# A gated scan with a mixture of experts: an earlier merge, masks with places in the order, another gather split

## The chip, the cores and the metric

The kernel runs on one core of a Trainium2 chip. The metric is device time in microseconds (us) of one launch. A core has a matrix engine (TensorE, PE in the profile, whose weight loads are shown as PEld), VectorE (DVE), ScalarE (ACT), GpSimd (POOL) and SyncE (SP, which here only issues DMAs).

## The reference

`x`, `r_gate` and `i_gate` are [4, 5056, 256] in fp32. First comes a gated linear recurrence along the sequence, then a top-1 mixture of experts over the 20,224 tokens that it gives:

```python
a = exp(8 * sigmoid(r_gate) * log(clip(sigmoid(a_param))))
u = sqrt(max(1 - a*a, 1e-6)) * sigmoid(i_gate) * x
h[t] = a[t] * h[t-1] + u[t]                      # for each of 4 sequences; y = h
logits = y @ w_gate                              # [20224, 8]
e = argmax(logits); gate = softmax(logits)[e]
for each expert: keep the 80 tokens with the largest gate
    out[token] = gate * (relu(y[token] @ w1[e]) @ w2[e])   # w1 256x1024, w2 1024x256
out of all other tokens = 0
```

At most 640 rows of the output are not zero.

## The kernel before

**Stages.** The tokens are cut into 40 units of 512 (unit 39 has 256). The outputs y of the recurrence stay on the chip, transposed, in the first 40 slots of one big tile `Y`; ten more slots and the free ones of the 40 hold what is loaded or under way. For each unit the program loads `r`, `i` and `x` (`Lr`, `Li`, `Lx`), transposes r on TensorE (`Tr`), makes the decay and the root on ScalarE and GpSimd, gates x, transposes it (`Tu`, two halves), multiplies by the norm on VectorE (`xg`) and scans on VectorE (`y`, two halves, line 173). Groups of four units get their logits on TensorE (`G`, for the last group `Ga` and `Gb`), and ten small stages (`R`, with a step number and a stage 0 to 9) turn logits into a table `rows`: one row for each of 16 slices of the tokens and each of the 8 experts, with the gate weight of each token that chose the expert. Step 4 is the last group but one, step 5 the last.

**The merge.** `P0` to `P3` (lines 324 to 328) keep the 8 largest of each 256 columns of the first 1024 columns of `rows`, 32 in all, in `cell`. `M0` (`merge(0)`, lines 334 to 338) takes the 16 largest of those 32 on VectorE and compares their positions with a list (line 338). `M1` and `M2` (lines 340 to 350) look up the columns on GpSimd. M0 keeps its positions in `pos`, which lies in slot 48 of `Y`; slot 48 also holds the loaded x of unit 38, which `Tu38.0` and `Tu38.1` read.

**The order.** The string `ORDER` (lines 35 to 64) lists all this, task by task, and each engine runs its own instructions in that order (`manual_schedule`, line 367). Its end, before:

```
u38.1 R3.8 y36.0 e38.1 Z y36.1 Tr39 R3.9 Tu37.1 tr39 xg37.0 G8 Z e39.1 q38.1 xg37.1 W0 s38.1 y37.0 q39.1 W1 y37.1 u39.1 P3 W2 Tu38.0 Tu38.1
s39.1 xg38.0 W3 R4.0 Tu39.0 xg38.1 R4.1 y38.0 W4 y38.1 Tu39.1 Z R4.2 Ga xg39.0 R4.3 xg39.1 y39.0 Z y39.1 W5 R4.4 R4.5 Gb Ca M0 W6 R5.0 R5.1
W7 R5.2 M1 R4.6 R5.3 R5.4 Z R5.5 R4.7 R5.6 M2 R4.8 Z R5.7 R5.8 R4.9 R5.9
```

`W` loads weights of the first two experts and `Z` zeroes 512 rows of the output; both are DMAs of SP's queue. What stands behind the list is placed by the compiler's scheduler. Among it are masks of constants (lines 383 to 390): `se` (written by GpSimd at line 383, finished by VectorE at 384 and 385), `iot` (386) and `comb` (389 and 390, VectorE).

**The choice.** Behind the list VectorE takes the 16 largest of the rest of `rows` (line 439), and lines 441 to 481 rank the candidates of the 16 slices against each other and turn the ranks into a table `chosen` of 80 tokens for each expert. Line 455 issues `WARM[0]` matmuls that compute nothing wanted (`keep_warm`, lines 418 to 420, tile `pd`).

**The experts.** `experts` (line 529) makes `col` (line 540), the columns of the 80 tokens of each expert in `Y`. For each expert, ScalarE, GpSimd and VectorE each load their share of the 80 columns into registers (`fetch`, line 553) and copy the tokens into `XG` one by one (`copies`, lines 559 and 560); `GATHER` gives the shares, 28, 24 and 28. Line 543 issues `WARM[1]` more empty matmuls in the meantime. Before the loop, VectorE turns a second table `pt` into `AT` (the gates) and `sidx` (the rows for the scatter) in six small instructions, lines 594 to 600. The loop (lines 603 to 616) gathers expert k+2, multiplies expert k+1 by w1 (`ph`, line 574) and expert k by w2 (`po`, line 576), interleaved, loads later weights as buffers come free, scales (line 584) and scatters (line 587).

Of the kernel before, what the change touches and what calls it, by code (L numbers as in the profile page):

```python
# [7 lines left out]
F32 = mybir.dt.float32  # L8
I32 = mybir.dt.int32
# [13 lines left out]
WARM = (7, 7)  # L23
GATHER = (28, 24, 28)
# [36 lines left out]
    u38.1 R3.8 y36.0 e38.1 Z y36.1 Tr39 R3.9 Tu37.1 tr39 xg37.0 G8 Z e39.1 q38.1 xg37.1 W0 s38.1 y37.0 q39.1 W1 y37.1 u39.1 P3 W2 Tu38.0 Tu38.1  # L61
    s39.1 xg38.0 W3 R4.0 Tu39.0 xg38.1 R4.1 y38.0 W4 y38.1 Tu39.1 Z R4.2 Ga xg39.0 R4.3 xg39.1 y39.0 Z y39.1 W5 R4.4 R4.5 Gb Ca M0 W6 R5.0 R5.1
    W7 R5.2 M1 R4.6 R5.3 R5.4 Z R5.5 R4.7 R5.6 M2 R4.8 Z R5.7 R5.8 R4.9 R5.9
# [18 lines left out]
def moe_kernel(ctx, tc, x, r_gate, i_gate, a_param, w_gate, w1, w2, out, capacity=80):  # L82
# [277 lines left out]
    def weights(w):  # L360
# [5 lines left out]
             'Tu': u_transposes, 'xg': normed, 'y': scan, 'G': logits, 'R': lambda s, k: stages[k](s), 'Ga': logits_first, 'Gb': logits_last, 'Ca': copy_first, 'P': cell_top, 'M': merge, 'W': weights, 'Z': lambda: zero_fill(1)}  # L366
# [14 lines left out]
    V = 2 * E  # L381
    se = lg[:, :P]; iot = lg[:, P:P + 80]
# [146 lines left out]
    def experts(arm):  # L529
        fstack = ExitStack()  # L530
        tstack = ExitStack()
        ps_t = tstack.enter_context(tc.tile_pool(name="ps_a" + arm, bufs=1, space=bass.MemoryType.PSUM))
# [8 lines left out]
        pt = ps_t.tile([CAP, 2 * E], F32, name="sel")  # L541
# [61 lines left out]
        for k in range(-1, E):  # L603
# [8 lines left out]
            if k >= 1: scatter(k - 1)  # L612
# [42 lines left out]
```

## Time and profile before

| | us |
|---|---|
| median of 3 runs (all of them) | 315.87 (315.51, 315.87, 318.1) |
| the profiled execution, its own time | 315.17 |
| its span, first to last instruction | 313.4 |
| busy in the span: PE, PEld | 217.6, 162.8 |
| DVE, ACT, POOL | 228.1, 233.0, 228.5 |

A page of the profile gives such sums, and other views list single instructions or groups of them by engine in order of time: start, duration, engine, line, operation, the tiles written and read with their shapes, how many there are (x8), and in brackets how long the engine had been idle before and what ended that. PEclk, the granted clock of TensorE, is given as a share of 2.4 GHz: 1.00 is that and 0.50 is 1.2 GHz. A TensorE row of fp32 matrices counts two instructions for a matmul and one for a transpose.

### The profile page before, as it was taken

Reading aid. Unit: us, or ns where it says so; the run is one execution under the profiler, and the core shown is the slowest. Engines: PE = TensorE matmul, PEld = TensorE weight load, DVE = VectorE, ACT = ScalarE, POOL = GpSimd, SP = SyncE. Lnnn points to the kernel's source line nnn. Section 1 sums busy time; section 2 is a strip of 40 time slices with the busy share of each in tenths; the row PEclk is TensorE's granted clock in tenths of the full one; section 3 lists DMA queues with packets and bytes.
Section 4 is the critical chain, followed back from the end, with each engine's and each line's share of the span. In section 5 each row is a group of like instructions: output and inputs, shape, how many; then the busy total and the mean of one; then the engine's idle time right before and its main releaser. Section 6 shows DMA issues by size and latency. Waiting matters only on the chain.

```text
span 313.4 us, 5668 instructions
## 1 busy us (share of the span) xinstructions
PE 217.6 (69%) x1404; PEld 162.8 (52%) x1404; DVE 228.1 (73%) x541; ACT 233.0 (74%) x463; POOL 228.5 (73%) x370
## 2 busy tenths in 40 slices
PE   3571677776456971988645957569618879999993
PEld 3451664426345241934633433344205669999993
DVE  1052699799989995999499996797968554666520
ACT  6999969999999996998899998898115353545400
POOL 2469298899999889799996999797257465654612
PEclk9958577959959997599795788756956598999999
DMA  7989999999999599989978999998999133999941
GB/s 254 405 310 391 395 337 413 407 390 391 413 405 351 188 386 389 395 310 367 393 291 321 349 383 338 383 330 278 360 423 335 55 101 131 331 341 344 315 128 29
DMA packets 32824, 100.73 MB, mean 321 GB/s; under 512 B 3744, under 2 KB 12576, under 8 KB 32160
## 3 DMA queue, kind: packets, MB, share of 16 engines
q1 hardware_dynamic: 32400, 99.64, 86.5%
q0 software_dynamic: 384, 0.66, 0.6%
q8 instruction: 13, 0.21, 0.3%
q14 instruction: 27, 0.22, 0.2%
HBM read 99.10 MB, written 21.36 MB: 384 GB/s over the span
## 4 chain that ended last, share of the span: by engine, by line
issue 25%; POOL 21%; DMA 14%; DVE 13%; PE 13%; ACT 9%; POOLq 2%; DVEq 1%; SPq 1%; ACTq 0%
DMA Y<-in_i_gate_dram 6%; POOL Y L143 6%; POOL Y L155 5%; DMA Y<-in_r_gate_dram 4%; POOL Y L154 4%; PE pr L126 4%; PE pl L236 4%; DVE pu L165 4%; ACT Y L140 3%; DMA Y<-in_x_dram 3%; POOL Y L560 3%; DVE Y L173 3%; PE pu L162 2%; ACT Y L128 2%; POOLq L553 2%
## 5 line engine op out<-in xcount | busy, mean ns | idle before, releaser
L173 DVE TENSOR_TENSOR_SCAN Y<-Y,pu 128x512 f32<-128x512 f32 (+4 forms) x86 | 97.2, 1170 | 0.0
L143 POOL TENSOR_TENSOR Y<-Y 128x1024 f32<-128x1024 f32 (+2 forms) x30 | 74.3, 2489 | 26.9 <-ACT Y L140 25.4
L162 PE MATMUL pu<-ident,Y 128*128 128x128 f32 x316 | 57.8, 322 | 39.3 <-DVE Y L173 24.2
L162 PEld LDWEIGHTS pu<-ident,Y 128*128 128x128 f32 x316 | 42.2, 166 | 65.6 <-issue 25.2
L126 PE MATMUL pr<-ident,Y 128*128 128x128 f32 x316 | 54.2, 332 | 30.3 <-DMA Y<-in_r_gate_dram 19.7
L155 POOL TENSOR_TENSOR Y<-Y 128x1024 f32<-128x1024 f32 (+2 forms) x25 | 68.7, 2747 | 4.5 <-DMA Y<-in_x_dram 2.5
L126 PEld LDWEIGHTS pr<-ident,Y 128*128 128x128 f32 x316 | 46.9, 175 | 33.9 <-issue 16.8
L165 DVE SCALAR_TENSOR_TENSOR pu<-Y,pu 128x512 f32<-128x512 f32 (+1 forms) x80 | 51.3, 676 | 14.5 <-ACT Y L146 7.5
L140 ACT ACTIVATE Y<-Y,tiny 128x512 f32<-128x512 f32 (+2 forms) x60 | 53.1, 943 | 1.5 <-DVE Y L157 1.2
L576 PE MATMUL po<-Y,rows 128*80 128x128 f32 x256 | 47.7, 279 | 0.0
L574 PE MATMUL ph<-Y 128*128 128x80 f32 x256 | 43.5, 262 | 2.2 <-DVE Y L560 2.0
L128 ACT ACTIVATE Y<-pr 128x1024 f32<-128x1024 f32 (+1 forms) x40 | 38.9, 1003 | 3.8 <-PE pr L126 3.8
L150 ACT ACTIVATE Y<-Y 128x1024 f32<-128x1024 f32 (+2 forms) x30 | 38.8, 1320 | 3.8 <-DMA Y<-in_i_gate_dram 3.2
L574 PEld LDWEIGHTS ph<-Y 128*128 128x128 f32 x256 | 38.6, 196 | 2.7 <-issue 2.7
L146 ACT ACTIVATE Y<-Y 128x1024 f32<-128x1024 f32 (+2 forms) x34 | 38.1, 1184 | 0.1
L157 DVE SCALAR_TENSOR_TENSOR Y<-Y 128x1024 f32<-128x1024 f32 x11 | 23.8, 2169 | 18.8 <-ACT Y L150 13.1
L559 ACT COPY Y<-Y 128x2 f32 x224 | 22.8, 191 | 18.7 <-issue 14.7
L560 POOL COPY Y<-Y 128x2 f32 x192 | 24.5, 197 | 15.3 <-issue 7.3
L236 PE MATMUL pl<-Y 128*32 128x512 f32 x144 | 34.2, 1078 | 0.6 <-ACT rows L312 0.6
L154 POOL TENSOR_SCALAR Y<-Y 128x1024 f32<-128x1024 f32 (+2 forms) x25 | 32.5, 1299 | 0.8 <-ACT Y L150 0.6
L576 PEld LDWEIGHTS po<-Y,rows 128*80 128x80 f32 x256 | 29.2, 155 | 0.0
L560 DVE COPY Y<-Y 128x2 f32 x224 | 24.9, 180 | 4.3 <-issue 4.3
(162 smaller groups left out, 171.0 us busy)
## 6 DMA issues: line engine op xcount, KB each, us to landing
Y<-in_r_gate_dram SPq DMA_DIRECT2D x39, 512.0 KB, 6.4
Y<-in_x_dram SPq DMA_DIRECT2D x39, 512.0 KB, 6.4
Y<-in_i_gate_dram SPq DMA_DIRECT2D x39, 512.0 KB, 6.6
out_dram<-out_dram SPq DMA_DIRECT2D x38, 512.0 KB, 6.9
Y<-in_moe_w_dram SPq DMA_DIRECT2D x32, 512.0 KB, 4.9
out_dram<-Y SPq DMA_DIRECT2D x1, 512.0 KB, 9.0
Y<-in_x_dram SPq DMA_DIRECT2D x1, 256.0 KB, 3.7
Y<-in_i_gate_dram SPq DMA_DIRECT2D x1, 256.0 KB, 4.3
```

The source lines that it names most:

```text
L126: nc.tensor.transpose(pr[:, h, b:nb * P:nb], rr[:, b, h * P:(h + 1) * P], ident)
L128: nc.scalar.activation(rslot(u), prs.pop(u)[:, :, :ntok(u)], AF.Tanh, scale=0.5)
L140: nc.scalar.activation(a[:, :, h], z[:, :, h], AF.Exp, scale=L[:, h:h + 1], bias=L[:, h:h + 1])
L143: nc.gpsimd.tensor_tensor(pair('r', u, m), a, a, op=ALU.mult)
L155: nc.gpsimd.tensor_tensor(v, i, v, op=ALU.mult)
L162: nc.tensor.transpose(pu[:, b:nb * P:nb], tmb('x', u)[:, b, h * P:(h + 1) * P], ident)
L165: nc.vector.scalar_tensor_tensor(pu, rslot(u)[:, h], 0.5e-3, pu, op0=ALU.max, op1=ALU.mult)
L173: nc.vector.tensor_tensor_scan(y[:, s0:s1], a[:, s0:s1], q[:, s0:s1], init, op0=ALU.mult, op1=ALU.add)
L236: nc.tensor.matmul(st['pl', step][32 * j:32 * j + 32, c0:c0 + len(units) * n // 4], wg[:, h, E - E * k:E - E * k + 32], Y[:, units[0]:unit ...
L560: else: eng.tensor_copy(dst, src)
L574: nc.tensor.matmul(ph[:, c % (FC // 2)], w1v(e1)[:, h, c * P:c * P + P], XG[:, e1, h], start=(h == 0), stop=(h == 1))
L576: nc.tensor.matmul(po[:, h, :P], h2T[:, c], w2v(e2)[:, c, h * P:h * P + P], start=(c == 0), stop=(c == FC - 1))
```

## The change

It does seven things, four in the list and three in the experts' part:

1. `M0`, without its last comparison, moves from behind `Ca` to in front of `xg38.0`. The comparison becomes `M3` and stands in front of `R5.0`.
2. `Ga` is cut in two, `Ga0` (units 36, 37) in front of `Tu39.1` and `Ga1` (unit 38) behind `xg39.0`.
3. The late stages of step 4 (`R4.6` to `R4.9`) move forward, in front of `R5.2` and `R5.4`.
4. The masks get places in the list (`I0`, `I1`, `I2`), and the two instructions of `comb` go from VectorE to GpSimd. `Z` moves a little.
5. `WARM` goes from (7, 7) to (7, 6).
6. The gather's split is 28, 28, 24 (ScalarE, GpSimd, VectorE) for experts 0 and 1, and 28, 24, 28 as before from expert 2 on.
7. The six instructions that make `AT` and `sidx` move from in front of the loop to behind VectorE's copies of expert 2; `pt` gets a PSUM bank of its own that lives as long as the loop.

```diff
-WARM = (7, 7)
-GATHER = (28, 24, 28)
+WARM = (7, 6)
+GATHER = ((28, 28, 24), (28, 24, 28))
...
-    u38.1 R3.8 y36.0 e38.1 Z y36.1 Tr39 R3.9 Tu37.1 tr39 xg37.0 G8 Z e39.1 q38.1 xg37.1 W0 s38.1 y37.0 q39.1 W1 y37.1 u39.1 P3 W2 Tu38.0 Tu38.1
-    s39.1 xg38.0 W3 R4.0 Tu39.0 xg38.1 R4.1 y38.0 W4 y38.1 Tu39.1 Z R4.2 Ga xg39.0 R4.3 xg39.1 y39.0 Z y39.1 W5 R4.4 R4.5 Gb Ca M0 W6 R5.0 R5.1
-    W7 R5.2 M1 R4.6 R5.3 R5.4 Z R5.5 R4.7 R5.6 M2 R4.8 Z R5.7 R5.8 R4.9 R5.9
+    u38.1 R3.8 y36.0 e38.1 Z y36.1 Tr39 R3.9 Tu37.1 tr39 xg37.0 G8 Z e39.1 q38.1 xg37.1 W0 s38.1 y37.0 q39.1 W1 y37.1 u39.1 P3 W2 Tu38.0 Tu38.1 M0
+    s39.1 xg38.0 W3 R4.0 Tu39.0 xg38.1 R4.1 y38.0 Z W4 Ga0 y38.1 Tu39.1 R4.2 xg39.0 Ga1 R4.3 xg39.1 y39.0 Z y39.1 W5 R4.4 R4.5 I0 Gb Ca W6 R4.6 R4.7 M3 R5.0 R5.1
+    W7 R4.8 R4.9 R5.2 R5.3 M1 R5.4 Z R5.5 R5.6 R5.7 I1 R5.8 R5.9 I2 Z M2 Z
...
-    def logits_first():
-        st['pl', LAST_STEP] = ps_r.tile([P, 2, C], F32, name="pr")[:, 0]
-        spread(LAST, list(range(4 * LAST, NU - 1)))
+    def logits_first(part):
+        if part == 0: st['pl', LAST_STEP] = ps_r.tile([P, 2, C], F32, name="pr")[:, 0]
+        spread(LAST, [NU - 2] if part else list(range(4 * LAST, NU - 2)))
...
             top16(cell, rows[:, NE:NE + K1], pos.bitcast(U32), cell)
+        if n == 3:
             nc.vector.tensor_tensor(where, pos.bitcast(U32).unsqueeze(2).broadcast_to([P, K1, NC]), nth.unsqueeze(1).broadcast_to([P, K1, NC]), op=ALU.is_equal)
...
+    def prepare(n):
+        if n == 0:
+            nc.gpsimd.iota(iot, pattern=[[1, 80]], base=0, channel_multiplier=0, allow_small_or_imprecise_dtypes=True)
+            nc.gpsimd.tensor_tensor(comb[:3 * V], ident[:3 * V, :V], ident[:3 * V, V:2 * V], op=ALU.add)
+            nc.gpsimd.tensor_tensor(comb[:3 * V], comb[:3 * V], ident[:3 * V, 2 * V:3 * V], op=ALU.add)
+        if n == 1:
+            nc.gpsimd.iota(se.bitcast(I32), pattern=[[1, P]], base=P, channel_multiplier=-1)
+        if n == 2:
+            nc.vector.tensor_scalar(se.bitcast(I32), se.bitcast(I32), E - 1, None, op0=ALU.bitwise_and)
+            nc.vector.tensor_scalar(se, se.bitcast(I32), 0.0, None, op0=ALU.is_equal)
...
-    nc.gpsimd.iota(se.bitcast(I32), pattern=[[1, P]], base=P, channel_multiplier=-1)
-    nc.vector.tensor_scalar(se.bitcast(I32), se.bitcast(I32), E - 1, None, op0=ALU.bitwise_and)
-    nc.vector.tensor_scalar(se, se.bitcast(I32), 0.0, None, op0=ALU.is_equal)
-    nc.gpsimd.iota(iot, pattern=[[1, 80]], base=0, channel_multiplier=0, allow_small_or_imprecise_dtypes=True)
-    nc.vector.tensor_tensor(comb[:3 * V], ident[:3 * V, :V], ident[:3 * V, V:2 * V], op=ALU.add)
-    nc.vector.tensor_tensor(comb[:3 * V], comb[:3 * V], ident[:3 * V, 2 * V:3 * V], op=ALU.add)
...
+        ps_s = fstack.enter_context(tc.tile_pool(name="ps_s" + arm, bufs=1, space=bass.MemoryType.PSUM))
...
-        pt = ps_t.tile([CAP, 2 * E], F32, name="sel")
+        pt = ps_s.tile([CAP, 2 * E], F32, name="pt")
...
-        nA, nP = [-(-CAP * g // 80 // 4) * 4 for g in GATHER[:2]]
-        SPAN = {'A': (nc.scalar, E_.Activation, 0, nA), 'P': (nc.gpsimd, E_.Pool, nA, nA + nP), 'V': (nc.vector, E_.DVE, nA + nP, CAP)}
+        cuts = [[-(-CAP * g // 80 // 4) * 4 for g in split[:2]] for split in GATHER]
+        nA = cuts[0][0]
+        def span(k, e):
+            a, p = cuts[0 if e < 2 else 1]
+            return {'A': (nc.scalar, E_.Activation, 0, a), 'P': (nc.gpsimd, E_.Pool, a, a + p), 'V': (nc.vector, E_.DVE, a + p, CAP)}[k]
...
-        nc.vector.tensor_copy(AT, pt)
-        nc.vector.tensor_scalar(tk, AT[:, :E], -1.0, 0.0, op0=ALU.add, op1=ALU.max)
-        nc.vector.tensor_scalar(un, tk, 10, 9, op0=ALU.logical_shift_right, op1=ALU.logical_shift_left)
-        nc.vector.tensor_tensor(tk, tk, un, op=ALU.subtract)
-        nc.vector.tensor_scalar(none, AT[:, :E], 0.0, 65536.0, op0=ALU.is_equal, op1=ALU.mult)
-        nc.vector.tensor_tensor(sidx, tk, none, op=ALU.add)
+        def slots_to_rows():
+            nc.vector.tensor_copy(AT, pt)
+            nc.vector.tensor_scalar(tk, AT[:, :E], -1.0, 0.0, op0=ALU.add, op1=ALU.max)
+            nc.vector.tensor_scalar(un, tk, 10, 9, op0=ALU.logical_shift_right, op1=ALU.logical_shift_left)
+            nc.vector.tensor_tensor(tk, tk, un, op=ALU.subtract)
+            nc.vector.tensor_scalar(none, AT[:, :E], 0.0, 65536.0, op0=ALU.is_equal, op1=ALU.mult)
+            nc.vector.tensor_tensor(sidx, tk, none, op=ALU.add)
...
             if e2 is not None:
                 copies('A', e2, 0, nA // 2); copies('P', e2); copies('V', e2)
+            if k == 0: slots_to_rows()
             if k >= 1: scatter(k - 1)
```

## Rows read from the trace of the kernel before

**Rows 1.** Stretches: length; PE, PEld, DVE, ACT, POOL busy (instructions); PEclk, DMA share, GB/s.

```profile
217.60:223.70 6.10, 4.79 (x36) 1.81 (x33) 6.09 (x12) 1.51 (x4) 1.37 (x8) 1.00 1.15 420
...
245.80:251.20 5.40, 5.40 (x14) 4.32 (x14) 3.27 (x29) 2.74 (x28) 3.07 (x24) 0.50 0.01 5
251.20:257.90 6.70, 4.48 (x37) 3.99 (x36) 4.07 (x34) 3.84 (x35) 4.47 (x35) 1.00 0.30 87
257.90:261.40 3.50, 3.50 (x20) 3.50 (x20) 2.15 (x19) 0.85 (x8) 2.26 (x19) 0.52 0.39 146
261.40:307.90 46.50, 46.50 (x460) 46.50 (x459) 22.60 (x166) 18.17 (x161) 21.36 (x123) 1.00 0.80 263
```

**Rows 2.** Timeline of VectorE, 216 to 232 us.

```profile
217.61 1.29 DVE L165 SCALAR_TENSOR_TENSOR pu<-Y,pu 128x512 f32<-128x512 f32 x2 [0.61 <-issue]
...
222.34 1.38 DVE L173 TENSOR_TENSOR_SCAN Y<-Y,pu 128x256 f32<-128x256 f32 x2
...
224.48 0.15 DVE L335 TENSOR_REDUCE Y<-Y 128x1 f32<-128x4 f32 x1
...
224.84 0.19 DVE L318 FIND_INDEX8 Y<-rows,Y 128x8 uint32<-128x32 f32 x1
...
225.94 0.69 DVE L338 TENSOR_TENSOR Y<-Y 128x512 f32<-128x512 uint32 x1
226.55 0.28 DVE L273 TENSOR_REDUCE Y<-pr 112x16 f32<-112x128 f32 x1
...
227.91 0.29 DVE L289 TENSOR_REDUCE Y<-pr 112x16 f32<-112x128 f32 x1
229.68 0.33 DVE L384 TENSOR_SCALAR lg<-lg 128x128 int32<-128x128 int32 x1 [1.48 <-POOL lg L383]
229.94 0.28 DVE L290 TENSOR_TENSOR Y<-pr,Y 112x128 f32<-112x128 f32 x1
...
230.35 0.21 DVE L385 TENSOR_SCALAR lg<-lg 128x128 f32<-128x128 int32 x1
...
231.87 0.43 DVE L317 MAX8 lg<-rows 128x8 f32<-128x256 f32 x1 [0.83 <-ACT rows L312]
```

**Rows 3.** Timeline of TensorE, 216 to 226 us.

```profile
216.72 1.44 PE L162 MATMUL pu<-ident,Y 128*128 128x128 f32 x10
...
224.90 0.70 PE L258 MATMUL pr<-ident,Y 128*112 128x128 f32 x4 [0.71 <-ACT Y L254]
```

**Rows 4.** Timeline of three engines at the first experts, 245 to 259 us.

```profile
245.77 5.94 PE L420 MATMUL pd<-Y,ident 128*128 128x256 f32 x14
247.67 3.07 POOL L560 COPY Y<-Y 128x2 f32 x24 [4.28 <-issue]
247.93 3.26 DVE L560 COPY Y<-Y 128x2 f32 x28 [2.13 <-issue]
...
251.10 0.16 DVE L594 COPY lg<-sel 80x16 f32<-80x16 f32 x1
...
251.92 3.77 PE L574 MATMUL ph<-Y 128*128 128x80 f32 x32 [0.21 <-issue]
251.94 3.29 POOL L560 COPY Y<-Y 128x2 f32 x24 [1.20 <-PE pd L420]
...
254.17 3.26 DVE L560 COPY Y<-Y 128x2 f32 x28 [1.87 <-issue]
...
257.69 0.42 PE L574 MATMUL ph<-Y 128*128 128x80 f32 x2 [2.00 <-DVE Y L560]
```

**Rows 5.** Timeline of GpSimd and VectorE: later gathers.

```profile
259.66 2.97 DVE L560 COPY Y<-Y 128x2 f32 x28
...
274.99 3.01 POOL L560 COPY Y<-Y 128x2 f32 x24 [0.60 <-issue]
```

**Rows 6.** Busy time by stretch, columns as in rows 1.

```profile
155.60:162.40 6.80, 3.53 (x30) 3.11 (x29) 5.95 (x9) 6.78 (x10) 6.80 (x3) 1.00 0.72 258
203.40:217.00 13.60, 10.46 (x44) 5.82 (x45) 11.89 (x16) 12.55 (x17) 13.03 (x14) 0.50 0.87 286
```

More of the change, by code (lines that the diff above doesn't have):

```diff
@@ L350, in merge @@
                 w //= 2
+    V = 2 * E
+    se = lg[:, :P]; iot = lg[:, P:P + 80]; small = lg[:, 208:512]; comb = small[:, 210:210 + V]
+    def prepare(n):
[8 more added lines that the diff above has]
+            nc.vector.tensor_scalar(se, se.bitcast(I32), 0.0, None, op0=ALU.is_equal)
     def w1v(e): return wbuf[e % 2][:, :2 * F].rearrange("p (h f) -> p h f", h=2)
@@ L365, in moe_kernel @@
              'Tr': r_transposes, 'tr': r_tanh, 'e': decay, 'q': square, 's': root, 'ti': i_tanh, 'u': gated, 'v': gated,
-             'Tu': u_transposes, 'xg': normed, 'y': scan, 'G': logits, 'R': lambda s, k: stages[k](s), 'Ga': logits_first, 'Gb': logits_last, 'Ca': copy_first, 'P': cell_top, 'M': merge, 'W': weights, 'Z': lambda: zero_fill(1)}
+             'Tu': u_transposes, 'xg': normed, 'y': scan, 'G': logits, 'R': lambda s, k: stages[k](s), 'Ga': logits_first, 'Gb': logits_last, 'Ca': copy_first, 'P': cell_top, 'M': merge, 'I': prepare, 'W': weights, 'Z': lambda: zero_fill(1)}
     with tc.manual_schedule(engines={E_.Activation, E_.PE, E_.DVE, E_.Pool}):
@@ L380, in moe_kernel @@
     KG, KF = -(-CAP // 8) * 8, 14
-    V = 2 * E
-    se = lg[:, :P]; iot = lg[:, P:P + 80]
-    nc.gpsimd.iota(se.bitcast(I32), pattern=[[1, P]], base=P, channel_multiplier=-1)
-    nc.vector.tensor_scalar(se.bitcast(I32), se.bitcast(I32), E - 1, None, op0=ALU.bitwise_and)
-    nc.vector.tensor_scalar(se, se.bitcast(I32), 0.0, None, op0=ALU.is_equal)
-    nc.gpsimd.iota(iot, pattern=[[1, 80]], base=0, channel_multiplier=0, allow_small_or_imprecise_dtypes=True)
-    small = lg[:, 208:512]
-    comb = small[:, 210:210 + V]
-    nc.vector.tensor_tensor(comb[:3 * V], ident[:3 * V, :V], ident[:3 * V, V:2 * V], op=ALU.add)
-    nc.vector.tensor_tensor(comb[:3 * V], comb[:3 * V], ident[:3 * V, 2 * V:3 * V], op=ALU.add)
     chosen = small[:3 * V, 0:CAP]
@@ L547, in experts @@
         XG = scr[:, :E * 2 * CAP].rearrange("p (e h s) -> p e h s", e=E, h=2)
-        nA, nP = [-(-CAP * g // 80 // 4) * 4 for g in GATHER[:2]]
-        SPAN = {'A': (nc.scalar, E_.Activation, 0, nA), 'P': (nc.gpsimd, E_.Pool, nA, nA + nP), 'V': (nc.vector, E_.DVE, nA + nP, CAP)}
+        cuts = [[-(-CAP * g // 80 // 4) * 4 for g in split[:2]] for split in GATHER]
[3 more added lines that the diff above has]
+            return {'A': (nc.scalar, E_.Activation, 0, a), 'P': (nc.gpsimd, E_.Pool, a, a + p), 'V': (nc.vector, E_.DVE, a + p, CAP)}[k]
         regs = {}
         def fetch(k, e):
-            eng, et, a, b = SPAN[k]
+            eng, et, a, b = span(k, e)
             regs[k] = nc.values_load_multi_w_load_instructions(col[e:e + 1, a:b], engines=[et], min_val=0, max_val=NU * 2 * C - C - 1,
@@ L555, in copies @@
         def copies(k, e, j0=0, j1=64):
-            eng, et, a, b = SPAN[k]
+            eng, et, a, b = span(k, e)
             for j in range(a + j0, min(b, a + j1)):
```

## The prediction

> **What bounds the kernel now.** I read the page's chain that ended last, then the busy times by stretch, then the timelines of the stretches that the change touches. From 261.4 to 307.9 us TensorE is busy for 46.50 of 46.50 us at a granted clock of 1.00 [rows 1]: once expert 1 is under way, nothing but its matmuls sets the end. So the last 50 us move as a block with the start of expert 1 (257.69, the first matmul that interleaves two experts [rows 4]) and with the clock of its first microseconds. Ahead of it there is one chain: VectorE's scans (busy 6.09 of 6.10 us from 217.6 to 223.7 [rows 1]), the last logits and their stages R5, the top 16 at 231.87 [rows 2], the ranking, the gather. Everything is to be priced by how far it moves 231.87 and then 257.69.
>
> **The early merge.** Its VectorE part (line 335 up to the comparison at line 338) takes 225.94 - 224.48 = 1.46 us [rows 2]. In its new place VectorE has a hole of 0.61 us, 217.00 to 217.61 [rows 2]. The first three instructions (224.48 to 224.84, 0.36 us) fit into it. The fourth, FIND_INDEX8, writes `pos` in slot 48, and must wait until unit 38's eight transposes have read that slot. They are the first eight of the ten in the row that ends at 218.16 [rows 3]; by the share of eight tenths, with the last two some 0.11 us apart, about 217.95. From the fourth instruction to the comparison were 224.84 to 225.94, 1.10 us. So xg38.0 starts near 219.05 instead of 217.61, and as the scans have no slack, all that follows is 1.45 us late (bounds: 0.85 if nothing waits, 1.65 if it waits for the tenth transpose). Queued behind the waiting instruction are the scans themselves; that is the price.
>
> What does it give back? Before, stage R5.2 started at 226.55 [rows 2], although its input from TensorE was there at 224.90 + 0.70 = 225.60 [rows 3]: VectorE was held by the merge and its comparison, 0.95 us. Now the last scan ends at 223.72 + 1.45 = 225.17, and the way from there over TensorE and ScalarE to the turned logits keeps its 225.60 - 223.72 = 1.88 us: 227.05. VectorE meanwhile has R4.4 (223.64 to 224.48, 0.84), a reciprocal (some 0.24, as small as line 385's 0.21) and the comparison (0.69), 1.77 us, done at 226.94. So R5.2 starts at 227.05, not 226.55: the move alone costs 0.5 us. Below, that cost is 0.1 us less than nothing (no wait for the transposes); above, 0.7.
>
> Cutting `Ga` in two costs nothing: TensorE is busy 4.79 of the 6.10 us [rows 1], and its last piece waits for the last scan either way.
>
> **The listed masks.** After the reduction that ends at 227.91 + 0.29 = 228.20, VectorE stands still for 1.48 us, in front of line 384, until GpSimd's iota of line 383 is done [rows 2]; the instruction that R5 needs, line 290, comes only then, at 229.94. Without the mask it can follow at 228.18, as such small instructions overlap by some 0.02: 1.76 us. Line 385 (0.21, at 230.35) also stands in the chain of R5, ahead of the reciprocal; with the overlap of its neighbours I count 0.13. Together 1.89 us go. In their new place the two take 0.33 + 0.21 = 0.54 us, inside the 0.83 us in which VectorE waits for ScalarE before 231.87 [rows 2]. Their iota stands ahead of M2's sums on GpSimd, and has from about 228 to 229 for itself. `comb` on GpSimd falls where it waits anyway. What is late next is the chain of R5 itself, which has nothing foreign left in it. If stage R4.9 now holds R5.3 up on ScalarE, some 0.3 us come back.
>
> Front: 0.5 - 1.89 = -1.4 us (from -2.0 to -0.9).
>
> **SP's queue.** A zero fill goes ahead of W4, and W4 to W7 come up to 1.45 us later, since they wait for slots that the last scans free. The DMA share is 0.01 from 245.8 to 251.2 [rows 1], so all of these have landed before the first expert, with 5 us to spare: 0.
>
> **The gather of experts 0 and 1.** All times in this part are on the clock of the trace before. VectorE: expert 0's 28 copies start at 247.93 and take 3.26, then six small instructions (from 251.10), then registers (1.87 idle), then 28 copies from 254.17 to 257.43, and TensorE follows 0.26 later, after 2.00 us of waiting [rows 4]. So VectorE is the last of the three gatherers: GpSimd ends expert 1 at 251.94 + 3.29 = 255.23, and ScalarE, whose share stays as it is, was not the last before either. The change takes from VectorE the six instructions (254.17 - 1.87 - 251.10 = 1.2 us), and two times four copies (0.116 each) and register loads: it would be done before 255.
>
> But GpSimd takes the copies. Its 24 of expert 0 take 3.07 (0.128 each) from 247.67; with four more registers (1.20 us for 24, so 0.2) and 28 copies (3.58) it ends at 251.45. Registers for 28 are 1.40, and 28 copies at the pace of expert 1 (3.29 for 24) 3.84: 256.69, and TensorE 0.26 later, 256.95. At the pace of expert 0 (3.58) it would be 256.69. I take 256.85: **expert 1 starts 0.85 us earlier**, and GpSimd is the bound in VectorE's place. Bounds: 0.3 earlier if both gathers have the slow pace and dearer loads, 1.2 if the four registers cost nothing.
>
> The Trainium skill speaks against more copies for GpSimd (SBUF — State Buffer, "Summary: rules for kernel authors"): where VectorE copies in a mode that uses both ports, the later of the two to issue blocks until the other is done. The rows deny it here: 24 GpSimd copies take 3.07 us wholly beside VectorE's [rows 4] and 3.01 at 274.99, where VectorE is mostly elsewhere [rows 5]. By the rule the copies of both would stand in one queue, the new split would change nothing, and the gain would be the six instructions' 1.2 us in place of 0.85.
>
> Expert 0 starts 0.2 earlier too: before, it followed the 14 empty instructions (5.94 us, to 251.71 [rows 4]); 12 take 5.09, and then GpSimd's 251.45 + 0.26 decides. The six moved instructions come behind VectorE's copies of expert 2 and cost nothing there: before, these end at 262.63 [rows 5] and would end sooner now, and the first user of `AT` runs after expert 1's matmuls, about 266.
>
> **The clock.** After the 2.00 us in which TensorE stood idle, it ran at 0.52, all but wholly the lower of its two levels (1.2 GHz), from 257.9 to 261.4: 20 instructions in 3.50 us, where the stretch behind does 460 in 46.50 [rows 1]. At that pace 20 take 2.0, so the low clock cost 1.5 us. Now expert 0's matmuls (3.77 us) end at 251.71 + 3.77 = 255.48 and the hole lasts to 256.85: 1.4 us instead of 2.0. Whether the clock stays up over it is the question on which most hangs. For it: from 155.6 to 162.4 TensorE was busy only 3.53 of 6.80 us, in small pieces, and kept 1.00 [rows 6]; here the two runs of matmuls beside the hole are dense. I take it that it stays: -1.5 (between 0 and -1.7).
>
> **Sum.** -1.4 - 0.85 - 1.5 = -3.75. The profiled execution took 315.17 (a span of 313.4 and 1.8 around it), so 311.4. The runs without a profile lie 0.3, 0.7 and 2.9 above it, the median 0.7; I add the 0.3 of the lowest and predict **311.7 us**, 1.3% under the median of 315.87. About 1% is what a measurement of this kernel can tell from no change, so this stands just beyond it.
>
> **Rivals.**
> - *The clock falls again* before expert 1. For it: it did so after 2.0 us. Then -2.25: 313.2, within 1%. Chance 0.17.
> - *The front gives little*: the merge waits for the tenth transpose (+0.2), and R4.8 and R4.9, now ahead of R5.3 on TensorE and ScalarE, hold that up (some 0.8 us by their durations if nothing overlaps). Front -0.4, sum -2.75: 312.7 to 312.8, within 1%. Against it: ScalarE idles there. Chance 0.12.
> - *The change does not do what it says*: another wait stands where line 384 stood, and GpSimd is as late as VectorE was. 315.0. Chance 0.05.
> - *Slower: the clock is not released before expert 0.* Two empty instructions fewer, and GpSimd 0.7 us later than before, open a hole of about 0.6 us in front of expert 0. If the clock is not at 1.00 when its first matmul starts, and stays down through both experts: from 203.4 to 217.0 it was 0.50 throughout although TensorE was busy 10.46 of 13.60 us [rows 6]. Expert 0's 3.77 us become some 7.2 (1.00 against 0.52), ending near 258.9, and expert 1's 64 instructions, at the 20 in 3.50 us of [rows 1], take 11.2: to 270.1, a little more if some records are missing. Before, it was 257.9 + 3.5 and 44 more at 460 in 46.50, 265.8. That is 4.3 to 5 us later, less the 1.4 in front: 318.4 to 319.2, taken as 319.0. Against it: before, the clock came back at 251.2 [rows 1], after 5.4 us of empty matmuls, and there are still 5.1. Chance 0.08.
>
> **The numbers.** The forecast has 0.58, and its own range is 310.6 to 312.7 (front -2.0, start -1.2, clock -1.7 on one side; front -0.9, start -0.5 on the other). With the first two rivals the range is 310.4 to 314.2; it leaves out the last two and a little below. Faster by over 1% (below 312.7) is the forecast with a little of the second rival, 0.59; within 1% 0.33; slower by over 1% 0.08.
>
> **What would show it.** VectorE: a wait in the merge, between its third and fourth instruction, xg38.0 near 219.05, R5.2 near 227.05, no hole in front of line 290, and the top 16 near 230.5. GpSimd's 28 copies of expert 1 as the last before TensorE's wait, some 1.4 us long. PEclk 1.00 in the first microseconds of expert 1. The forecast is wrong if TensorE is at 0.50 there, if the scans are late by more than 1.65 us, or if a part of the block behind 261.4 waits for weights.

## The result, and the profile after

The kernel after takes 314.37 us (median of 9 runs), the kernel before, run beside it, 318.1: a ratio of 0.9892, with a 95% interval of 0.9853 to 0.9932, so 1.08% faster. A ratio here counts only the runs within 1.5% of the fastest of their kernel; the means that follow take in all. The forecast was 311.7 us and its range ended at 314.2. Over everything that was run later, the kernel before has a mean of 318.0 us (61 runs, 314.9 to 321.2) and the kernel after 314.5 (21 runs, 309.6 to 318.2): 3.5 us less, give or take 1.0.

The execution of the change that was profiled took 317.41 us (span 315.4), longer than that of before (315.17, 313.4). So the two traces can't be compared by their ends. I set marks in the span instead: **A**, the first transpose of unit 38 (216.72 before, 220.89 after; nothing ahead of it is changed), **B**, the top 16 of the rest, **C**, VectorE's instruction that makes the columns of the tokens, **D**, the first matmul that interleaves two experts, **S**, the last scatter, **E**, the end of the span (known to 0.1 us).

VectorE after, 221 to 236 us, and from TensorE the eighth of unit 38's transposes with the two behind it, at 221.71 (start, duration, engine, line, operation, tiles, count, idle time and what ended it):

```profile
221.08 0.14 DVE L335 TENSOR_REDUCE Y<-Y 128x1 f32<-128x4 f32 x1
...
221.52 0.09 DVE L318 MATCH_VALUE_LOAD Y<-rows,Y 128x8 f32 x1 [0.20 <-DMA Y<-in_moe_w_dram]
221.60 0.18 DVE L318 FIND_INDEX8 Y<-rows,Y 128x8 uint32<-128x32 f32 x1
221.71 0.49 PE L162 MATMUL pu<-ident,Y 128*128 128x128 f32 x3
...
222.52 1.27 DVE L165 SCALAR_TENSOR_TENSOR pu<-Y,pu 128x512 f32<-128x512 f32 x2
...
227.45 1.39 DVE L173 TENSOR_TENSOR_SCAN Y<-Y,pu 128x256 f32<-128x256 f32 x2
...
231.24 0.29 DVE L273 TENSOR_REDUCE Y<-pr 112x16 f32<-112x128 f32 x1 [0.86 <-PE pr L258]
...
232.55 0.29 DVE L289 TENSOR_REDUCE Y<-pr 112x16 f32<-112x128 f32 x1
232.87 0.29 DVE L290 TENSOR_TENSOR Y<-pr,Y 112x128 f32<-112x128 f32 x1
...
233.90 0.22 DVE L363 TENSOR_SCALAR lg<-lg 128x128 int32<-128x128 int32 x1
234.16 0.23 DVE L364 TENSOR_SCALAR lg<-lg 128x128 f32<-128x128 int32 x1
234.81 0.43 DVE L317 MAX8 lg<-rows 128x8 f32<-128x256 f32 x1 [0.43 <-ACT rows L312]
```

The merge now stands ahead of xg38.0 (line 165). Its wait in front of the lookup is 0.20 us, and xg38.0 starts 1.63 us behind A; before it was 0.89 [rows 2, 3]. Lines 289 and 290 follow each other without the 1.48 us of [rows 2], and the two mask instructions (lines 363 and 364) lie where VectorE would wait for ScalarE. B stands at A + 13.92 instead of A + 15.15.

The three engines at the first experts, after:

```profile
250.76 2.82 DVE L568 COPY Y<-Y 128x2 f32 x24 [1.89 <-issue]
255.19 0.63 DVE L568 COPY Y<-Y 128x2 f32 x5 [1.61 <-issue]
256.13 2.23 DVE L568 COPY Y<-Y 128x2 f32 x19 [0.32 <-issue]
...
251.00 3.54 POOL L568 COPY Y<-Y 128x2 f32 x28 [4.69 <-issue]
255.95 0.19 POOL L568 COPY Y<-Y 128x2 f32 x1 [1.42 <-issue]
256.37 3.41 POOL L568 COPY Y<-Y 128x2 f32 x27 [0.23 <-issue]
...
248.79 5.28 PE L424 MATMUL pd<-Y,ident 128*128 128x256 f32 x12
254.59 3.80 PE L582 MATMUL ph<-Y 128*128 128x80 f32 x32 [0.52 <-POOL Y L568]
259.83 0.45 PE L582 MATMUL ph<-Y 128*128 128x80 f32 x2 [1.45 <-POOL Y L568]
```

GpSimd is now the last of the three gatherers (256.37 + 3.41 = 259.78; VectorE ends at 258.36, ScalarE at 258.60), and TensorE's hole is 1.45 us where [rows 4] had 2.00. The stretches behind it, after (columns as in [rows 1]):

```profile
254.60:258.30 3.70, 3.70 (x32) 3.63 (x32) 2.80 (x24) 2.77 (x27) 2.12 (x17) 1.00 0.03 10
259.80:263.30 3.50, 3.47 (x21) 3.47 (x22) 3.08 (x27) 1.52 (x14) 2.27 (x19) 0.61 0.47 152
263.30:311.20 47.90, 47.19 (x461) 46.96 (x460) 22.34 (x164) 18.17 (x161) 22.78 (x134) 0.99 0.79 256
```

This is the row that goes against the forecast: expert 0 ran at a granted clock of 1.00 (2.4 GHz), and the first 3.5 us of expert 1 at 0.61, mostly the lower level (1.2 GHz, from 260.55 to 263.96), 21 instructions. It is the same loss as the 0.52 of [rows 1].

All marks, from the profiled execution of each kernel that was run (us; the edits are told below):

| kernel | A | A to B | B to C | C to S | S to E | A to E |
|---|---|---|---|---|---|---|
| before | 216.72 | 15.15 | 13.70 | 63.55 | 4.28 | 96.68 |
| before_again | 219.11 | 15.01 | 13.63 | 64.67 | 5.38 | 98.69 |
| before_third | 218.64 | 15.02 | 13.68 | 63.55 | 4.11 | 96.36 |
| before_fourth | 220.34 | 15.01 | 13.63 | 61.91 | 5.01 | 95.56 |
| after | 220.89 | 13.92 | 13.83 | 62.64 | 4.12 | 94.51 |
| after_again | 217.73 | 13.78 | 13.61 | 62.59 | 5.09 | 95.07 |
| after_third | 220.76 | 13.92 | 13.85 | 62.66 | 4.81 | 95.24 |
| after_fourth | 219.19 | 13.77 | 13.62 | 62.74 | 5.48 | 95.61 |
| after_fifth | 219.77 | 13.77 | 13.92 | 62.63 | 4.31 | 94.63 |
| front_only | 217.53 | 13.81 | 13.61 | 63.38 | 5.77 | 96.57 |
| tail_only | 218.57 | 15.01 | 13.98 | 62.59 | 5.25 | 96.83 |
| split_old | 218.23 | 13.79 | 13.62 | 61.18 | 5.58 | 94.17 |
| rows_first | 218.64 | 13.78 | 13.68 | 61.02 | 5.38 | 93.86 |
| hole_filled | 219.44 | 13.79 | 13.62 | 61.04 | 4.11 | 92.56 |
| filled_again | 218.39 | 13.78 | 13.62 | 61.00 | 4.11 | 92.51 |
| before_filled | 218.03 | 15.01 | 13.68 | 61.92 | 5.56 | 96.17 |
| merge_late | 219.41 | 12.66 | 15.53 | 62.53 | 4.97 | 95.69 |
| merge_back | 220.40 | 13.62 | 13.67 | 61.01 | 5.40 | 93.70 |
| merge_mid | 220.54 | 13.40 | 13.88 | 62.65 | 4.23 | 94.16 |
| best | 216.94 | 13.59 | 13.61 | 61.01 | 4.05 | 92.26 |

A to C falls into two groups, by the list of the order alone: 28.6 to 29.0 with the old one, 27.4 to 27.8 with the new; with the merge at other places it is 28.19 (merge_late) and 27.2 to 27.3 (merge_back, merge_mid, best). C to S falls into four, by the gather and the clock: 61.9, or 63.4 to 63.6 where the clock fell, with the old experts' part, and 61.0 to 61.2 or 62.5 to 62.7 with the new. Only before_again lies outside, at 64.67: there the clock fell 1.14 us ahead of D and stayed down twice as long as at expert 1 in the others.

### The profile page after: what moved, and what is told of

Same layout as the page of the kernel before. It is cut to its first block, busy times and chain, and to the rows that moved or that the text cites. A ratio compares the mean times of both kernels' runs of the same rounds, so it can differ in the third digit from the quotient of the medians.

```text
span 315.4 us, 5694 instructions
## 1 busy us (share of the span) xinstructions
PE 217.3 (69%) x1418; PEld 164.4 (52%) x1418; DVE 226.9 (72%) x531; ACT 232.8 (74%) x463; POOL 230.4 (73%) x380
## 4 chain that ended last, share of the span: by engine, by line
issue 23%; POOL 20%; DMA 19%; ACT 13%; PE 12%; DVE 8%; POOLq 3%; SPq 1%; DVEq 0%; ACTq 0%
DMA Y<-in_i_gate_dram 7%; POOL Y L155 5%; POOL Y L568 5%; DMA Y<-in_r_gate_dram 4%; DMA Y<-in_x_dram 4%; POOL Y L143 4%; ACT Y L140 4%; POOL Y L154 4%; PE pr L126 3%; ACT Y L146 3%; DVE Y L173 2%; PE pu L162 2%; PE pl L236 2%; ACT Y L128 2%; POOLq L561 2%
## 5 line engine op out<-in xcount | busy, mean ns | idle before, releaser
L126 PE MATMUL pr<-ident,Y 128*128 128x128 f32 x316 | 55.5, 337 | 32.8 <-DMA Y<-in_r_gate_dram 29.5
L162 PEld LDWEIGHTS pu<-ident,Y 128*128 128x128 f32 x316 | 43.3, 167 | 64.6 <-issue 35.3
L126 PEld LDWEIGHTS pr<-ident,Y 128*128 128x128 f32 x316 | 47.6, 177 | 36.7 <-issue 24.8
L568 POOL COPY Y<-Y 128x2 f32 x200 | 25.6, 196 | 15.8 <-issue 7.9
L568 DVE COPY Y<-Y 128x2 f32 x216 | 23.4, 174 | 4.7 <-issue 4.7
```

What stands on the lines that cost most here:

```text
L126: nc.tensor.transpose(pr[:, h, b:nb * P:nb], rr[:, b, h * P:(h + 1) * P], ident)
L162: nc.tensor.transpose(pu[:, b:nb * P:nb], tmb('x', u)[:, b, h * P:(h + 1) * P], ident)
L568: else: eng.tensor_copy(dst, src)
```

## The experiments

**The level of the kernel before.** Three more profiled executions, no edit.

> The kernel before, unchanged, a second profile. Four marks in each trace: A, the first transpose of unit 38; B, the top 16 of the rest (the first MAX8 behind the list); C, the columns; D, the first matmul of expert 1; and the end E. Before they were A 216.72, A to B 15.15, B to C 13.70, C to D 12.12, D to E 55.71 us; after, A 220.89, then 13.92, 13.83, 11.19, 55.57. Theory (the load-bound part ahead of A, which the change does not touch, differs from run to run by some us): A lies anywhere from 216 to 221, and A to E is again 96.7 within 0.5. Rival (the change itself makes A late): A within 0.5 of 216.7.

> The kernel before, a third profiled execution. If the first profiled execution (315.17) was a quick one by the part that the change does not touch: the first transpose of unit 38 stands at 217 to 221 us, and from there to the end of the span it takes 96.7 to 98.7 us as in the first two, whatever the whole time is. If the level of the kernel before is the 315.2 to 315.9 that the prediction started from: 315 to 316.

> A fourth profiled execution of the kernel before, with the same two readings: 96.7 to 98.7 us from the first transpose of unit 38 to the end, and a whole time that depends on when that transpose comes; or 315 to 316 us.

They took 319.57, 316.81 and 317.6 us. The first one, of which the prediction was made (315.17), is among the quickest of all 61. From A to E it is not quick (96.68 against 98.69, 96.36 and 95.56); it is quick because A came early, at 216.72. The expectation that A to E is 96.7 within 0.5 (96.7 to 98.7 in the last two) was missed in all three: C to S, which takes in the clock, varies by 2.8 us and S to E by 1.3. A follows unit 39's transposes of `r` by 5.6 us in all nine executions of the two kernels, and in eight of them these wait for a load of `r`. TensorE in front of unit 39's `Tr` (line 126), in the kernel before:

```profile
211.11 1.09 PE L126 MATMUL pr<-ident,Y 128*128 128x128 f32 x4 [1.06 <-ACT Y L140]
```

and in the kernel after, whose code is the same there:

```profile
215.28 1.09 PE L126 MATMUL pr<-ident,Y 128*128 128x128 f32 x4 [3.54 <-DMA Y<-in_r_gate_dram]
```

Here it waits 3.54 us for `r`; in before_again the wait for the same load is 2.74, in before_fourth 2.68. In after_fourth and after_fifth it is only 0.4 to 0.5, with A at 219.19 and 219.77, so waits further ahead have a part in it. The start of everything that the change touches moves by up to 4 us from one execution to the next.

**Halves of the change.** `front_only` has the new list and the old experts' part, `tail_only` the reverse:

```diff
 # front_only
-WARM = (7, 6)
-GATHER = ((28, 28, 24), (28, 24, 28))
+WARM = (7, 7)
+GATHER = ((28, 24, 28), (28, 24, 28))
+        slots_to_rows()
         tstack.close()
...
-            if k == 0: slots_to_rows()
 # tail_only: ORDER, logits_first, merge and the masks behind the list as before
```

> The new list of the order (early merge, cut logits, late stages of step 4, listed masks) with the old experts' part (7 empty matmuls, split 28, 24, 28, scatter rows ahead of the loop). Theory of parts that add up: A to B 13.9, B to C 13.8, C to D 12.1, D to E 55.7; 1.1 us less than before from A to E, a ratio near 0.996. Rival (the front's gain is lost again at the experts, as a wait there is what counts): A to B 13.9, but C to D over 13.

> The old list with the new experts' part. Theory of parts that add up: A to B 15.1, B to C 13.7, C to D 11.2, D to E 55.6 if the clock falls before expert 1 and 54.0 if it stays up; 0.9 or 2.5 us less than before, a ratio of 0.997 or 0.992. Rival (the two halves need one another): C to D over 11.8.

Ratios to the kernel before: front_only 0.9937 (0.9897 to 0.9977), tail_only 0.9849 (0.9793 to 0.9905). By the marks the front takes 28.6 to 28.9 us from A to C down to 27.42, and leaves the rest (hole 2.31 us); the tail brings D from C + 12.12 to C + 11.18, and leaves the front. The two halves don't touch each other. Both lost the clock as expert 1 began, 1.5 us behind D (front_only) and 0.1 ahead of it (tail_only).

**Which gather edit does it.** `split_old` keeps the six instructions behind VectorE's copies but gathers by 28, 24, 28; `rows_first` keeps the new split but makes the six in front of the loop.

```diff
 # split_old
-GATHER = ((28, 28, 24), (28, 24, 28))
+GATHER = ((28, 24, 28), (28, 24, 28))
 # rows_first
+        slots_to_rows()
         tstack.close()
...
-            if k == 0: slots_to_rows()
```

> The kernel after, with the split 28, 24, 28 for all experts: of the gather's edits only the later scatter rows are left. Theory (either of the two edits alone takes VectorE out of the way, and GpSimd at 28 copies is as late as VectorE at 28): C to D 11.0 to 11.2, as after. Rival (the split is what gains): C to D 11.6 or more.

> The kernel after, with the six instructions of the scatter rows back in front of the loop: of the gather's edits only the split is left. VectorE then has 24 copies, 1.2 us, registers and 24 copies, done some 10.3 us behind C, where GpSimd is done 10.95 behind it. Theory as for the old split: C to D 11.2, as after. Rival (the later rows are what gains): C to D 11.9 or more.

D stands at C + 11.39 and C + 11.20, against 11.19 with both edits and 12.12 with neither. TensorE's wait in split_old, then in rows_first:

```profile
257.03 0.42 PE L582 MATMUL ph<-Y 128*128 128x80 f32 x2 [1.73 <-DVE Y L568]
```

```profile
257.30 0.45 PE L582 MATMUL ph<-Y 128*128 128x80 f32 x2 [1.28 <-POOL Y L568]
```

Either edit alone gives nearly all of it: with the old split VectorE is still last, with the new one GpSimd, and once GpSimd is last the six instructions are worth nothing. Both executions kept the clock, although the hole of split_old is longer than that of the change.

**The clock.** First the change twice more, and again, without an edit:

> The changed kernel, unchanged, a second profile. S is the last scatter (the last indirect DMA of GpSimd): from D to S the first two traces of before have 51.4 and 52.5 us, the kernel with the filled hole 49.8, and from S to the end E 4.3 and 5.4 and 4.1. Theory (the edits' own gains are fixed, A and S to E vary from run to run): A to B 13.9 within 0.15, C to D 11.2 within 0.1, D to S 51.4 if the clock falls before expert 1 and 49.8 if it stays up, A anywhere from 216 to 221. Rival (A at 220.9 belongs to the change): A above 220.5 again.

> The change once more, beside the version with the middle merge and the filled hole, on the same chip. If the clock's fall differs from execution to execution, the stretch from the columns to the last scatter is either 61.1 (it stays up) or 62.6 (it falls); ratio to the kernel before 0.983 to 0.992, and 0.5 to 1% slower than the other version.

> The change, a fourth profiled execution. Without a filled hole the clock has fallen in front of or during the first two experts in 4 of 5 executions with the old experts' part and in 6 of 9 with the new one. If the shorter hole makes a fall rarer, the columns to the last scatter take 61.0 us here and in the next one; if it makes no difference, 62.5 in at least one of the two. First transpose of unit 38 to the columns: 27.4 or 27.75 us by the front's own clock; with the new list it has had no other value.

> A fifth profiled execution of the change, with the same readings: 61.0 or 62.5 us from the columns to the last scatter, 27.4 or 27.75 us ahead of them.

after_again had a ratio of 0.9829 (0.9705 to 0.9954), after_third of 0.9773 (0.9702 to 0.9845); the second rests on two of its six runs, and the median of all six, 314.56, is 0.988 of the 318.52 of the kernel before. C to S is 62.6 to 62.7 in all five executions of the change: it lost the clock every time, in after, after_third and after_fifth within 0.8 us behind the first matmul of expert 1, in after_again and after_fourth already during expert 0. TensorE in after_fourth:

```profile
246.58 2.86 PE L424 MATMUL pd<-Y,ident 128*128 128x256 f32 x12
252.51 5.97 PE L582 MATMUL ph<-Y 128*128 128x80 f32 x34 [3.08 <-POOL Y L568]
```

The six empty matmuls (twelve instructions), which filled 5.28 us in the first execution, ran at 2.4 GHz from the start here and were over after 2.86; then TensorE stood for 3.08 us in front of expert 0, and its windows show 0.78 for expert 0 and 0.52 behind it. A fixed number of empty matmuls covers a fixed time only if the clock is known. The other way round, the kernel before kept its clock once, in before_fourth, over a hole of 2.40 us:

```profile
254.93 3.77 PE L574 MATMUL ph<-Y 128*128 128x80 f32 x32 [0.97 <-DVE lg L594]
261.10 0.42 PE L574 MATMUL ph<-Y 128*128 128x80 f32 x2 [2.40 <-DVE Y L560]
...
261.10:264.60 3.50, 3.50 (x35) 3.50 (x36) 1.95 (x17) 1.07 (x9) 2.27 (x19) 1.00 0.29 104
```

Then the hole was taken away, by three empty matmuls behind those of expert 0 (four in the kernel before), into columns of the `po` bank that nothing reads:

```diff
 # hole_filled, filled_again (FILL = 3, on the change); before_filled (FILL = 4, on the kernel before)
             if e2 is not None:
                 ...
                 po = pos[e2]
+            if e2 == 0 and half == 0:
+                for _ in range(FILL): nc.tensor.matmul(po[:, 0, P:P + 256], ident[:, :CAP], vvf, start=True, stop=True)
```

> The kernel after, with three empty matmuls (six instructions of 256 columns) behind expert 0's, in unused columns of the bank of expert 0's second product. If the clock falls because TensorE waits for GpSimd's copies of expert 1, it is at 1.00 through expert 1 now: D to E 54.0 in place of 55.57, C to D the same 11.2, and a ratio some 0.005 below the 0.989 of the change when the clock falls in most runs of it. Rival (the clock falls for another reason, or falls in few runs only): D to E 55.6, or 54.0 with a ratio of 0.989.

> The change with its hole filled, once more. If the hole is what drops the clock, the clock stays up again and the columns to the last scatter take 61.0 us; if the clock's fall has another cause, 62.5.

> The kernel before with one thing added: four empty matmuls behind those of expert 0, where TensorE stands idle for 2.0 to 2.4 us. If the hole is what drops the clock, the granted clock stays at 2.4 GHz through the start of expert 1, and the columns to the last scatter take 62.0 us (63.5 less the 1.5 that the prediction put on the low clock): ratio 0.995. If the clock falls for another reason: 63.5 and no difference.

TensorE and the windows behind it in filled_again:

```profile
251.72 3.80 PE L585 MATMUL ph<-Y 128*128 128x80 f32 x32 [1.39 <-POOL Y L569]
255.35 1.46 PE L580 MATMUL po<-Y,ident 128*80 128x256 f32 x6
256.97 0.45 PE L585 MATMUL ph<-Y 128*128 128x80 f32 x2 [0.16 <-POOL Y L569]
...
257.00:260.50 3.50, 3.50 (x35) 3.50 (x36) 3.13 (x28) 1.74 (x15) 2.33 (x19) 1.00 0.46 147
```

The hole is 0.16 us, D is not later (C + 11.18), the clock stays at 1.00, 35 instructions instead of 21 run in the same 3.5 us, and C to S is 61.0. hole_filled has a ratio of 0.9799 (0.9753 to 0.9846) to the kernel before, before_filled 0.9887 (0.9805 to 0.997). In all four executions with a filled hole (best, below, is the fourth) the clock stayed; with open holes it fell in 4 of 5 executions with the old experts' part and in 8 of 11 with the new one (in two of these, after_again and after_fourth, during expert 0).

The traces show more of when it falls, and that four of four says less than it seems. In each trace the instants at which the granted clock changes lie on a regular grid, to 0.001 us, and where a point of the grid lies against D differs from one execution to the next. With the hole in front of expert 1 open, the clock fell in all nine executions in which a point lies between 0.19 us ahead of D and 1.50 behind it, among them before (0.31 behind), after_third (0.25) and after_fifth (0.23). It stayed in four of the five in which the next point lies later, 1.74 to 2.74 behind D (before_fourth, merge_back, rows_first and split_old); in the fifth, before_again, it fell at a point 1.14 ahead of D, in a hole of 2.43. In hole_filled, filled_again and best the next point lies 2.30, 2.76 and 1.82 behind D, so these three would probably have kept the clock over an open hole too. Only in before_filled does one lie where the clock fell in all the others, 0.26 behind D, and there it stayed:

```profile
258.80:262.30 3.50, 3.46 (x34) 3.49 (x35) 1.90 (x17) 1.20 (x11) 2.26 (x20) 1.00 0.39 138
```

So an open hole of 1.4 to 2.4 us in front of expert 1 is what makes the fall possible, by one execution with the hole filled against three with a point at nearly the same place, and where the grid lies decides whether it comes. The hole in front of expert 0 is not filled by these edits (it is 1.47 and 1.39 us in hole_filled and filled_again), so a fall like those of after_again and after_fourth remains possible.

The Trainium skill says why that can be (TensorE: Matmul & The Clock Gate, "What's actually happening"): the chip's look at TensorE's activity runs freely and does not start with the kernel's work, so the point at which the clock changes shifts from run to run. before_third and before_fourth agree with that: the same code, a hole of 2.40 us in both, and C to S of 63.55 in one and 61.91 in the other, with the next point of the grid 1.05 and 1.74 us behind D.

**Where the merge belongs.** Three other places for it, on the change:

```diff
 # merge_back:  ... Tu38.0 Tu38.1            ... R4.6 R4.7 M0 M3 R5.0 R5.1
 # merge_late:  M0 there too;  I1 R5.4 Z R5.5 R5.6 R5.7 M3 R5.8 R5.9 I2 M1 Z M2 Z
 # merge_mid:   M0 there too;  W7 R4.8 R4.9 I1 R5.2 R5.3 M3 M1 R5.4 Z R5.5 ...
```

> The change with one thing undone: the merge (all but its comparison) goes back to where it stood, in front of R5.0, with the comparison behind it. The scans should then end as before, 6.9 us behind unit 38's first transpose instead of 7.95. If the early place is worth what the prediction said of it (it costs 0.5 by itself), the stretch from that transpose to the top 16 of the rest gets shorter than the change's 13.8 us: 13.3. If the early place pays because VectorE has the merge out of the way when the last logits come, it gets no shorter or longer: 13.6 to 14.2. The stretch from there to the columns stays 13.6 in both, since GpSimd's look-ups come no later than before.

> The kernel after, with the merge (M0) back behind the last scan, in front of R5.0, and its comparison (M3) behind R5.7, where VectorE waits for TensorE and ScalarE. Theory (the early merge delays the scans by 0.75 to 0.95 us, and costs more there than it takes away from R5): the last scan ends 6.9 behind A in place of 7.95, R5.2 starts near 9.5 in place of 10.0 to 10.35, A to B 13.2 in place of 13.9, B to C the same 13.8. Rival (the merge is better early): A to B 13.9 or more, or B to C longer by what A to B gains, as the look-up on GpSimd comes late.

> The merge in front of R5.0, its comparison and the first look-up between R5.3 and R5.4, GpSimd's iota for the mask ahead of R5.2. The scans end early (6.9) as in the kernel before, and the comparison fills a time in which VectorE waits for ScalarE. If the look-up is early enough for GpSimd: first transpose to the top 16 12.9 us, from there to the columns 13.6, together 26.6 against the change's 27.4. If GpSimd is late again, as with the late merge: 12.9 and 14.5 to 15.5, together no better than 27.4.

merge_back: A to B 13.62, between the two expectations, and 0.15 to 0.30 shorter than with the early merge; B to C is unchanged. So the early place by itself costs 0.15 to 0.3 us and buys nothing, as far as one execution of merge_back can tell. merge_late (0.9951, 0.9908 to 0.9994) has by far the shortest A to B, 12.66, and gives it back behind B: GpSimd's product (line 345) and the sums behind it wait for the late comparison (line 339), which ends at 231.84; the view names line 363, the next instruction of VectorE, which ends at 231.98.

```profile
228.93 0.24 POOL L344 TENSOR_TENSOR tiny<-tiny,Y 128x32 f32<-128x32 f32 x1
231.16 0.68 DVE L339 TENSOR_TENSOR Y<-Y 128x512 f32<-128x512 uint32 x1
231.99 1.09 POOL L345 TENSOR_TENSOR Y<-Y,tiny 128x512 f32<-128x512 f32 x1 [2.82 <-DVE lg L363]
...
232.42 0.75 DVE L364 TENSOR_SCALAR lg<-lg 128x128 f32<-128x128 int32 x1
```

merge_mid has the comparison where VectorE waits for ScalarE (0.34 us there), and R5.2 starts at A + 9.15, 0.76 earlier than in merge_back. But A to B is 13.40, not the 12.9 expected (and A to C 27.28, not 26.6), since a later instruction of VectorE got longer beside GpSimd's sums:

```profile
232.24 0.73 POOL L349 TENSOR_TENSOR Y<-Y 128x256 f32<-128x256 f32 x1
...
232.28 0.83 DVE L304 TENSOR_TENSOR Y<-Y 112x128 f32<-112x128 f32 x1
```

Line 304 takes 0.29 us in merge_late, where GpSimd is idle at that time; here it is issued 0.04 us behind the start of a GpSimd sum of 0.73 and ends 0.83 later, as if it had begun only when most of that was done. In merge_back it takes 0.44, in after_again, after_fourth and after_fifth 0.57 to 0.58: in all of these it is issued during one of GpSimd's sums and ends 0.15 us behind the end of that sum. In the first execution of the change it is issued as a sum ends, takes 0.29, and GpSimd's next sum takes 0.52 instead of 0.38 to 0.39. The Trainium skill has a rule for such pairs (SBUF — State Buffer, "Who interferes with whom"): a VectorE instruction with two inputs in SBUF contends with a GpSimd instruction that reads SBUF, and the later of the two waits. These durations, 0.83 among them, agree with it in the main, though the 0.15 is less than the 0.29 that line 304 takes alone.

**Both together.** `best` is merge_mid with the hole filled.

> The middle merge together with the three empty matmuls behind those of expert 0. If the hole in TensorE's work is what drops the clock, the granted clock stays at 2.4 GHz through the start of expert 1, and the columns to the last scatter take 61.0 us as with the filled hole; with the middle merge's 26.6 the kernel is 0.8 us faster than the filled change and about 2 us faster than the change: ratio to the kernel before 0.975 to 0.982. If the clock falls for another reason, 62.5 and a ratio near 0.985.

313.48 us (median of 6), ratio 0.9857 (0.9807 to 0.9908). Clock up, C to S 61.01, A to E 92.26, the shortest of all. But the ratio is above the 0.975 to 0.982 expected, and A to C is 27.20 against 27.40 and 27.41 with the filled hole alone: the middle merge was worth 0.2, not 0.8. In whole times it can't be told from hole_filled (312.89). Either beats the kernel before; that it beats the change is shown for the stretch from A to E (92.3 to 92.6 against 94.5 to 95.6), while the whole times (313.3 as the mean of 13 runs with the filled hole, 314.5 of the 21 of the change) lie too close for their spread.

## Why the prediction was right or wrong

**Two steps failed: the base, and the clock.** The one that put the time outside the range: "I add the 0.3 of the lowest and predict 311.7 us". Three runs were shown, 315.51, 315.87 and 318.1; I took the profiled 315.17 for the level, and the lowest run for the offset. The level is 318.0. The forecast of -3.75 from there is 314.3, and 314.37 was measured. The range took in the unknown costs of the change, and nothing for the level, although one of three runs lay 2.9 us above the profile. That agreement is luck in part: of the -3.75 the clock's -1.5 came in no trace of the change, and the traces show 1.9 us in all (below).

**The front, forecast -1.4 (-2.0 to -0.9).** A to C is 28.71 before (mean of four) and 27.60 after (mean of five): -1.1, in the range. Inside it terms were mis-sized, in opposite directions. "must wait until unit 38's eight transposes have read that slot": the wait is 0.20 us, and the lookup starts at 221.60, ahead of the eighth transpose at 221.71 (`pos` lies in columns 256 to 271 of the slot, and only the second of the eight reads these). So xg38.0 comes 0.74 later instead of 1.45, and the early place costs 0.15 to 0.3 in place of 0.5. The way from the last scan over TensorE to the turned logits, 1.88 in the forecast, is 1.88 in three of the five executions and 2.30 in after and after_third, where the granted clock had fallen to 1.2 GHz by 8.9 us behind A. R5.2 then starts at A + 9.93 or A + 10.35 (forecast 10.33). The listed masks, counted at 1.89, show without the early merge in merge_back, whose A to B is 1.39 shorter than the 15.01 of the kernel before (the cut of `Ga` and the late stages of step 4 are in that too): the stall in front of line 290 is worth what was forecast (line 289 to 290 was 2.03 us [rows 2] and is 0.32), but R5.2 comes 0.1 to 0.2 later there (9.91 behind A, before 9.83 and three times 9.70), and from line 290 to B it takes 2.09 instead of 1.93, as line 304 got longer beside GpSimd. B was put at 230.5, which is A + 13.78; the five executions have 13.77 to 13.92, which is luck in part, since R5.2 varies by 0.42 and line 304 takes most of that back where R5.2 is early.

**The gather, forecast -0.85 (-1.2 to -0.3).** C to D went from 12.12 to 11.19 (11.48 in after_again, where expert 0 ran slowly): -0.93. GpSimd's way from the end of expert 0's copies to that of expert 1's is 259.78 - 254.54 = 5.24 us, the 1.40 + 3.84 of the forecast. The 28 copies of expert 0 take 3.54 beside VectorE's (3.58 forecast), so the copies of the two engines do not block each other. The rule of the Trainium skill that the prediction weighed (SBUF — State Buffer, "Summary: rules for kernel authors") thus does not show for these copies. That GpSimd becomes the bound was forecast; that either edit alone suffices was not.

**The clock, forecast -1.5 (-1.7 to 0).** "I take it that it stays" is the second step that failed: it fell in all five profiled executions of the change, so the first rival (the clock falls again, -2.25 in all, chance 0.17) is what the traces show: A to S, 92.1 to 90.3, is -1.9 us. "The two runs of matmuls beside the hole are dense" was no reason; a hole of 1.4 us can cost the clock as one of 2.0 can, and one of 2.4 can leave it. A term that comes whole or not at all, and changes between executions of one kernel, should have entered with its chance (over open holes the clock stayed in 4 of 16 executions), not in full. The price itself was right: with the hole filled, C to S is 61.0 instead of 62.65, 1.65 us.

**What stays open.** By the traces from A to E the change is worth 1.8 us, by all runs 3.5, give or take 1.0. The five executions of the change with a trace are on the slow side of its runs (mean 316.5; the other sixteen 313.9). A alone is 1.0 us later in these five traces than in the four of the kernel before (219.67 against 218.70), ahead of all that the change touches. If the others kept the clock, more would be explained, but over open holes only 4 of 16 executions did; no trace of the others is there to show it.

**The slower rival** (the clock not released before expert 0) did not come in its form: in both cases where expert 0 ran slowly (after_again and after_fourth) the clock was up at its first matmul and fell 1.5 and 2.1 us later, behind a hole of 1.39 and 3.08 us in front of it. And it made nothing slower than a fall at expert 1: C to S is 62.59 and 62.74.

## What to carry to other kernels

Before a forecast rests on one profiled execution, set it beside the other runs: when they spread by more than the change is worth, forecast the difference, put it on the middle of the runs, and give the level its own share of the range. A hole of one or two microseconds between dense runs of matmuls is worth filling with empty ones even where nothing waits for less, as this cost nothing here, and the fall that it can keep away costs 1.65 us; count how many fill it at the clock that really holds there. Of two edits that shorten parallel arms, only the one on the arm that ends last pays, so give each a run of its own.

## What the runs showed of the hardware that I had not expected

The granted clock after the same hole differs between executions of one kernel (2.40 us: 1.00 once, 1.2 GHz another time), with the place of the instants at which it can change. A VectorE instruction of 0.29 us took 0.83 beside GpSimd's sums (line 304), and in merge_late line 364 took 0.75 instead of 0.23 beside line 345, while GpSimd's 28 copies of two elements kept their pace beside VectorE's. And the time up to A varies by 4 us, in part with the arrival of `r`.
